# Fused chunked attention and gated MLP: other ranks in the second phase of an instruction planner

## The chip, the cores and the metric

The kernel runs on one core of a Trainium2 chip. A core has five engines with instruction queues of their own: PE (TensorE, matmuls into PSUM), DVE (VectorE), ACT (ScalarE), POOL (GpSimd) and SP (SyncE, which issues most of the DMAs here). They wait for each other by semaphores only, and each works through its own queue in order. The metric is the device time of one execution in microseconds (us), as the median over runs.

## The reference

For each of 4 batches and 8 heads (768 positions, head width 64), queries in chunks of 32 attend to 8 memory keys and to a window of 56 keys around the chunk. The result, as x of 768 x 512 per batch, goes through a gated MLP:

```
h = np.maximum(x @ w_in, 0.0)                      # 512 -> 1024
u, v = (h[..., :d_ff // 2], h[..., d_ff // 2:])
v_n = (v - mu) / np.sqrt(var + 1e-06)              # over the 512 features
v_s = np.einsum('ts,bsd->btd', w_spatial, v_n) + b_spatial[None, :, None]
out = (u * v_s) @ w_out                            # 512 -> 512
```

## The kernel before, in words

Every large product is made of three matmuls with operands that are split into a rounded high part and the low rest (high x high, low x high, high x low). ACT writes the high part (a CAST), DVE the low one (a subtraction of the high part from the operand).

**First phase.** Attention runs in 24 units of 128 queries, and among them the products with w_in (`f`). v_n and u go out to DRAM (`vn_far`, `u_far`).

**Second phase.** For each batch b, `spatial(b)` forms the 768 x 768 product with w_spatial and `ffn_o(b)` the product with w_out. Each is done on quarters of its operands by seven products instead of eight, p1 to p7 (the function `product`). A left operand is either a quarter itself (p1, p2, p4) or a sum of quarters (`sm`, function `total`, on DVE: s1 and s2 for p5 and p6, s3 for p7, s4 for p3). `left` then makes the operand `op` out of it: `high` on ACT, `low` on DVE. The steps of a spatial product run as p1, p2, p6, p5, p7, p4, p3, each of two parts of nine matmuls of 384 columns; those of ffn_o as p1, p6, p5, p7, p4, p3, p2, each of three parts of six matmuls of 256 columns. Between batches they alternate: after p1 (and p2) of spatial(b) comes ffn_o(b-1), then the rest of spatial(b).

The bank `y` gathers p1, p6, p7 and p4 one on the other: after each of them something has to read it before PE may add the next. In spatial these readers are: a bias add on DVE and a copy to `st` on ACT after p1, copies on ACT after p6 and p7, a multiplication into `ug` on DVE after p4. Results of p2, and of p5 with p3, lie in banks of the ring `f` (three of them), and DVE joins them to the copies in `st`. POOL adds a bias step to some of the `st` tiles and multiplies them into the gate tiles `ug` (the loaded u). The gated `ug` quarters are the operands of ffn_o.

**w_out.** It comes as float64, and `from_f64` turns it into float32 tiles `big` during the first phase. Then `right_hand` makes the seven right operands of ffn_o for each half c: two direct ones, and two sums on POOL per temporary tile `st` (eight 128 x 256 sums in all, L916); `split` writes a high part on ACT (L887) and a low part on DVE (L891) for each. `w_out_pair(c, rank, load_rank)` does this for one half.

**What sets the order.** No engine's order is written down. Each piece is given to `Plan.op` with an engine, an estimated duration, the keys it reads and writes, and a rank. `Plan.order` walks through estimated time: for each engine it takes, of the operations that are ready, the one that could start first, and among equal starts the one with the lowest rank. The result is one fixed list per engine. In the second phase ranks are `1e3 + seq[0]`, where `seq[0]` counts the steps given to the plan so far; PE's are `1e4 + seq[0]`. The two calls of `w_out_pair` stand right behind the first step of spatial(0).

Of the kernel before, what the change touches and what calls it, by code (L numbers as in the profile page):

```python
# [28 lines left out]
class Plan:  # L29
# [38 lines left out]
    def order(self):  # L68
        ops = self.ops
        users = [[] for _ in ops]  # L70
        left = [len(o[3]) + len(o[8]) for o in ops]
        for n, o in enumerate(ops):
            for d in (*o[3], *o[8]):
                users[d].append(n)
        end, ready = self.end, self.start = {}, {}
        free = {e: 0.0 for e in ENGINES}
        pipe, landed = self.landing, []
        lone = both = 0.0
        taken = {ring: [] for ring in self.rings}
        waiting = {e: [] for e in ENGINES}  # L80
        for n, o in enumerate(ops):
            if not left[n]:
                ready[n] = 0.0
                waiting[o[0]].append(n)
        out, spares = [], []
        while len(out) < len(ops):
            best = None
            for e, ns in waiting.items():
                pick = None
                for n in ns:  # L90
                    t = max(free[e], ready[n], free["POOL"] if ops[n][9] else 0.0, lone if e == "POOL" else 0.0)
                    if ops[n][5]:
                        t = max(t, self.held_by(landed, ops[n][5], 0))
                    for s in ops[n][7]:
                        have = taken[s[0]]
                        if s not in have and len(have) >= self.rings[s[0]]:
                            old = self.slots[have[-self.rings[s[0]]]]
                            t = max([t] + [end.get(m, 1e9) for m in old])
                    if t >= 1e9:
                        continue  # L100
                    late = max(t, free[e])
                    c = (late, ops[n][4], n)
                    if pick is None or c < pick:
                        pick = c
                if pick and (best is None or pick < best[0]):
                    best = (pick, e)
            (t, _, n), e = best
            if e == "PE" and self.idle and 9.0 < t < 36.0:
                spare = int((t - max(free[e], 9.0) - 0.7) / 0.225)
                if spare > 0:  # L110
                    spares.append((max(free[e], 9.0), -spare))
            _, us, _, _, _, mb, tail, held, _, alone, drag, shared = ops[n]
            beside, pace = {"DVE": (free["POOL"] if shared else 0.0, 1.75), "POOL": (both, 1.4)}.get(e, (0.0, 1.0))
            if beside > t:
                us += min((beside - t) * (1 - 1 / pace), us * (pace - 1))
            for s in held:
                if s not in taken[s[0]]:
                    taken[s[0]].append(s)
            waiting[e].remove(n)
            free[e] = t + us  # L120
            if alone:
                lone = t + us
            if shared:
                both = t + us
            if mb:
                pipe = max(pipe, t + us) + mb * drag / self.rate
                end[n] = pipe + self.landing
                landed.append((end[n], mb))
            else:
                end[n] = t + us + tail  # L130
            self.start[n] = t
            out.append((t, n))
            for m in users[n]:
                left[m] -= 1
                if not left[m]:
                    ready[m] = max([self.start[d] + ops[d][1] if ops[d][0] == ops[m][0] == "PE" else end[d] + self.lat for d in ops[m][3]]
                                   + [self.start[d] for d in ops[m][8]])
                    waiting[ops[m][0]].append(m)
        return [n for _, n in sorted(out + spares)]
# [19 lines left out]
def tile_chunked_attention_gmlp(  # L159
# [380 lines left out]
    seq = [0]  # L540
# [112 lines left out]
    def product(kind, b, steps, halves, chunks, width, parts, N, right, right_keys, sum_eng, done):  # L653

        tag = (kind, b)
        (a11, k11), (a12, k12), (a21, k21), (a22, k22) = halves
        W = chunks * width

        def total(name, in0, in1, o, keys, to=None):
            rank = 1e3 + seq[0]  # L660
            sm = ("sm", (*tag, to or name))

            def go():
                if to is None:
                    alloc("sm", sm[1], [P, W], F32)
                a = t_[sm].rearrange("p (s n) -> p s n", s=chunks)
                {"DVE": nc.vector, "POOL": nc.gpsimd}[sum_eng].tensor_tensor(a, in0(), in1(), op=o)  # L667
            op(sum_eng, dve(W) if sum_eng == "DVE" else pool_(W), go, r=keys, w=[sm], rank=rank,
               shared=sum_eng == "DVE")
            return (lambda: t_[sm].rearrange("p (s n) -> p s n", s=chunks)), [sm]  # L670

        def left(name, of, keys):
            rank = 1e3 + seq[0]
            ok = ("op", (*tag, name))

            def half(x):
                return t_[ok][:, x].rearrange("p (s n) -> p s n", s=chunks)

            def high():
                alloc("op", ok[1], [P, 2, W], F32R)  # L680
                nc.scalar.copy(half(0), of())  # L681

            def low():
                nc.vector.tensor_tensor(half(1), of(), half(0).bitcast(F32), op=ALU.subtract)  # L684
            op("ACT", act(W), high, r=keys, w=[(*ok, "h")], rank=rank)
            op("DVE", dve(W), low, r=[*keys, (*ok, "h")], w=[(*ok, "l")], rank=rank, shared=True)
            return half, [(*ok, "h"), (*ok, "l")]

        def blocks(name, a, bi, bank, first):
            half, keys = a  # L690
            for p in range(parts):
                n = (*tag, bank, p)
                ring = "y" if bank == "y" else "f"
                cols = slice(p * P, (p + 1) * P)

                def go(n=n, ring=ring, cols=cols):
                    o = alloc(ring, n, [P, N], F32, psum=True) if first else t_[ring, n]
                    m = 0
                    for s in range(chunks):
                        h, l_ = half(0)[:, s, cols], half(1)[:, s, cols]  # L700
                        rh, rl = right(bi, 0, s), right(bi, 1, s)
                        for x, y in ((h, rh), (l_, rh), (h, rl)):
                            m += 1
                            nc.tensor.matmul(o, x, y, start=first and m == 1, stop=m == 3 * chunks,  # L704
                                             skip_group_check=True)
                op("PE", 1e-3 * 3 * chunks * (0.4375 * N + 6.5), go, r=[*keys, *right_keys(bi)], w=[(ring, n)],
                   rank=1e4 + seq[0], tail=0.25)
                done(name, p, (ring, n))
            seq[0] += 1

        direct = {"p1": ("a11", a11, k11), "p2": ("a12", a12, k12), "p4": ("a22", a22, k22)}
        s1 = s2 = None
        for name in steps:
            if s1 is None and name not in direct:
                s1 = total("s1", a21, a22, ALU.add, [*k21, *k22])
                s2 = total("s2", s1[0], a11, ALU.subtract, [*s1[1], *k11])
            of = direct.get(name)
            if name == "p5":
                of = ("s1", *s1)
            elif name == "p6":  # L720
                of = ("s2", *s2)
            elif name == "p7":
                of = ("s3", *total("s3", a11, a21, ALU.subtract, [*k11, *k21]))
            elif name == "p3":
                of = ("s4", *total("s4", a12, s2[0], ALU.subtract, [*k12, *s2[1]], to="s2"))
            i, bank = {"p1": (0, "y"), "p2": (1, "x"), "p3": (2, "z"), "p4": (6, "y"), "p5": (3, "z"), "p6": (4, "y"),
                       "p7": (5, "y")}[name]
            blocks(name, left(*of), i, bank, name in ("p1", "p2", "p5"))
            yield
# [236 lines left out]
    for x in FIRST:  # L966
        if x[0] == "w":
            c = int(x[1])
# [31 lines left out]
    for b in range(B + 1):  # L1000
        if b < B:
            rank = 300.0 + 10 * b
# [6 lines left out]
                next(spatials[b])  # L1009
            if b == 0:  # L1010
                for c in range(2):
                    w_out_pair(c, 1e3 + seq[0], 180.0)
        if b:
            o = ffn_o(b - 1)
            if b == B - 1:
# [57 lines left out]
```

## Time and profile before

| | |
|---|---|
| median of 3 runs (range) | 378.03 us (375.24 to 379.47) |
| the profiled execution, its own time | 377.27 us |
| span of the profile in it | 375.5 us |
| PE busy in the span | 357.4 us, 95% |
| DVE, ACT, POOL busy | 290.7, 187.1, 157.0 us |

The profile shows one execution on the chip by the hardware profiler; its times count from the first instruction. Matmuls are pipelined and their ends are modelled, so the start of the next block tells better than the end of one when PE was through. "Granted clock" is the share of the full TensorE clock (2.4 GHz) that the matmuls got; the other level is 1.2 GHz. A number of DMAs, loads of weights into PE and semaphore work stand in queues of their own. A wait is put down to the release that came last.

### The profile page before, as it was taken

To read this page: it belongs to the slowest core of one execution; us is meant where nothing else is said; L and a number is where in the kernel's file an instruction comes from. 1 tells how busy PE (TensorE), PEld (TensorE's weight loads), DVE (VectorE), ACT (ScalarE), POOL (GpSimd) and SP (SyncE) were. 2 spreads that over 40 slices of the span, in tenths; PEclk is the share of its full clock that TensorE was granted. 3 is DMA by queue.
4 is the path that set the end of the run, shared out by engine and by line. 5 is a ranking of instruction groups with operands and counts; after the bars stand their busy time and mean duration, and the time that the engine had idled before them with its cause. 6 is when DMAs were issued, how large, how long until landed. Compare 5 with 4: busy or idle time off the path is not lost.

```text
span 375.5 us, 11922 instructions
## 1 busy us (share of the span) xinstructions
PE 357.4 (95%) x5026; PEld 330.2 (88%) x5026; DVE 290.7 (77%) x480; ACT 187.1 (50%) x334; POOL 157.0 (42%) x154
## 2 busy tenths in 40 slices
PE   2799999999999999999999997999999999999996
PEld 2787888988989889889798996999999999999995
DVE  3799977669577498574796789699969996898893
ACT  3568552555555446454473345336533742743271
POOL 6164643366286067620033486452256024207410
PEclk9999999999999999999999999899999999999999
DMA  8999987885796894977844444404720662140015
GB/s 203 259 237 251 226 248 246 257 250 161 216 261 200 237 265 140 244 191 223 264 138 147 176 160 178 161 1 150 265 93 1 185 236 86 65 147 1 0 44 168
DMA packets 47557, 65.52 MB, mean 174 GB/s; under 512 B 4496, under 2 KB 38928, under 8 KB 47504
## 3 DMA queue, kind: packets, MB, share of 16 engines
q1 hardware_dynamic: 46848, 64.44, 57.8%
q8 instruction: 39, 0.64, 0.7%
q10 hardware_dynamic: 656, 0.33, 0.3%
q14 instruction: 14, 0.11, 0.1%
HBM read 45.88 MB, written 18.87 MB: 172 GB/s over the span
## 4 chain that ended last, share of the span: by engine, by line
PE 79%; DVE 10%; DMA 6%; ACT 2%; SPq 1%; issue 1%; POOL 0%; DVEq 0%; ACTq 0%; POOLq 0%
PE y L704 21%; PE f L704 14%; PE f L554 11%; PE f L555 11%; PE f L556 10%; PE sx L412 8%; DMA big<-in_moe_w_in_dram 4%; PE xt L516 2%; PE pt L500 2%; DVE op L684 2%; DVE sm L667 2%; DMA vmain<-in_v_dram 2%; DVE wout L891 1%; SPq L281 1%; ACT op L681 1%
## 5 line engine op out<-in xcount | busy, mean ns | idle before, releaser
L704 PE MATMUL y<-wsp,op 128*128 128x384 f32 x288 | 53.9, 344 | 3.1 <-ACT op L681 2.1
L704 PEld LDWEIGHTS y<-wsp,op 128*128 128x128 f32 x288 | 51.4, 193 | 3.9 <-ACT op L681 2.4
L758 POOL TENSOR_TENSOR ug<-st,ug 128x384 f32<-128x384 f32 x24 | 34.5, 1452 | 34.8 <-DVE st L750 30.8
L554 PE MATMUL f<-x,win_h 128*128 128x384 f32 x128 | 45.8, 358 | 0.0
L556 PE MATMUL f<-x,win_h 128*128 128x384 f32 x128 | 43.2, 337 | 0.0
L555 PE MATMUL f<-x,win_l 128*128 128x384 f32 x128 | 43.1, 337 | 0.0
L554 PE MATMUL f<-win_h,x 128*128 128x512 f32 x96 | 41.0, 427 | 0.0
L704 PE MATMUL f<-wsp,op 128*128 128x384 f32 x216 | 39.4, 336 | 0.0
L555 PE MATMUL f<-win_h,x 128*128 128x512 f32 x96 | 38.0, 396 | 0.5 <-DVE x L525 0.3
L556 PE MATMUL f<-win_l,x 128*128 128x512 f32 x96 | 37.7, 393 | 0.0
L764 POOL TENSOR_TENSOR st<-st,bias 128x384 f32<-128x384 f32 x14 | 18.0, 1286 | 47.2 <-ACT st L744 33.5
L704 PEld LDWEIGHTS f<-wsp,op 128*128 128x128 f32 x216 | 37.6, 188 | 0.0
L684 DVE TENSOR_TENSOR op<-sm,op 128x768 fp32r<-128x768 f32 x32 | 34.0, 1066 | 3.8 <-ACT op L681 3.3
L704 PE MATMUL y<-wout,op 128*128 128x256 f32 x288 | 36.0, 281 | 0.4 <-DVE op L684 0.4
L452 DVE TENSOR_TENSOR xs<-sx,rec 128x512 f32<-128x512 f32 x24 | 16.5, 689 | 25.4 <-PE sx L412 25.2
L704 PEld LDWEIGHTS y<-wout,op 128*128 128x128 f32 x288 | 34.8, 188 | 1.0 <-DVE op L684 0.8
L590 POOL TENSOR_TENSOR rstd<-ve,mhalf 128x1 f32<-128x1 f32 x24 | 14.5, 604 | 49.4 <-DVE ve L586 47.5
L681 ACT CAST op<-sm 128x768 fp32r<-128x768 f32 x32 | 26.3, 837 | 16.5 <-DVE sm L667 16.1
L412 PEld LDWEIGHTS sx<-kmain,q 64*32 64x32 f32 x1536 | 17.2, 108 | 14.3 <-issue 11.7
L578 ACT ACTIVATE st<-f 128x512 f32<-128x512 f32 x24 | 14.3, 598 | 28.3 <-PE f L556 27.9
L412 PE MATMUL sx<-kmain,q 64*32 64x64 f32 x1536 | 21.1, 229 | 7.5 <-ACT kmain L397 7.5
L391 POOL COPY vmain<-memv 8x1024 f32<-8x1024 f32 x22 | 23.8, 1085 | 9.9 <-PE sx L412 7.7
(86 smaller groups left out, 777.5 us busy)
## 6 DMA issues: line engine op xcount, KB each, us to landing
vmain<-in_v_dram SPq DMA_DIRECT2D x48, 128.0 KB
u_far<-uo SPq DMA_DIRECT2D x32, 192.0 KB
vn_far<-st SPq DMA_DIRECT2D x24, 256.0 KB
vr<-vn_far SPq DMA_DIRECT2D x8, 768.0 KB
ug<-u_far SPq DMA_DIRECT2D x16, 384.0 KB
q<-in_q_dram SPq DMA_DIRECT2D x11, 512.0 KB
vmain<-in_v_dram SPq DMA_DIRECT2D x47, 96.0 KB
out_dram<-ot SPq DMA_DIRECT2D x33, 128.0 KB
```

The source lines that it names most:

```text
L391: ins = {"DVE": nc.vector, "POOL": nc.gpsimd}[eng].tensor_copy(to, of)
L412: ins = nc.tensor.matmul(o, w_, m, start=True, stop=True, skip_group_check=True)
L452: nc.vector.tensor_tensor(xs.rearrange("p t r d -> p r t d"), t_["sx", i][:, :, 1], rec.rearrange("p t r -> p r t").unsqueeze(3).broadcast ...
L554: nc.tensor.matmul(o, lh, rh, start=(j == 0), stop=False)
L555: nc.tensor.matmul(o, ll, rh, start=False, stop=False)
L556: nc.tensor.matmul(o, lh, rl, start=False, stop=(j == len(pairs) - 1))
L590: nc.gpsimd.tensor_tensor(a, t_["ve", i], mhalf, op=ALU.pow)
L681: nc.scalar.copy(half(0), of())
L684: nc.vector.tensor_tensor(half(1), of(), half(0).bitcast(F32), op=ALU.subtract)
L704: nc.tensor.matmul(o, x, y, start=first and m == 1, stop=m == 3 * chunks, skip_group_check=True)
L758: nc.gpsimd.tensor_tensor(g, t_[st(x)], g, op=ALU.mult)
L764: {"DVE": nc.vector, "POOL": nc.gpsimd}[eng].tensor_tensor(a, a, bias[:, 1], op=ALU.add)
```

## The change

Three edits.

```diff
@@ Plan.order: for each engine, the choice among ready operations
-                pick = None
+                pick, soon = None, []
...
                     late = max(t, free[e])
                     c = (late, ops[n][4], n)
+                    soon.append(c)
                     if pick is None or c < pick:
                         pick = c
+                if pick and e in ('ACT',) and pick[1] >= 1e3:
+                    pick = min((c for c in soon if c[0] <= pick[0] + 0.1), key=lambda c: (c[1], c[2]))
@@ product, total
-            rank = 1e3 + seq[0]
+            rank = 1e3 + seq[0] - 2
@@ main loop, b == 0
-                    w_out_pair(c, 1e3 + seq[0], 180.0)
+                    w_out_pair(c, 1e3 + seq[0] + (3, 5)[c], 180.0)
```

The sums of quarters (`total`) rank two steps earlier. The two halves of the w_out conversion rank three and five steps later. And where the plan would give ACT an operation of the second phase, it now takes the lowest rank among all that could start within 0.1 us of the first. No instruction is added, removed or resized. The instruction lists are the same up to the entry into the second phase (all attention, all products with w_in); from there on they differ in order. The lines of the changed file stand 3 higher.

**DVE, entry of the second phase.** Before, behind the bias add to the first part of p1 (y_3935). `sm_4083` is the sum s3, the operand of p7; L891 writes low parts of w_out, L750 joins p2 to its copy.

```order
L891 TENSOR_TENSOR wout_3958<-big_3358,wout_3958 128x256
L891 TENSOR_TENSOR wout_3958<-big_3373,wout_3958 128x2x256
L769 TENSOR_TENSOR y_3969<-y_3969,bias_100 128x384
L891 TENSOR_TENSOR wout_3958<-big_3459,wout_3958 128x256
L891 TENSOR_TENSOR wout_3958<-st_3961,wout_3958 128x2x256
L891 TENSOR_TENSOR wout_3958<-big_3495,wout_3958 128x2x256
L891 TENSOR_TENSOR wout_3958<-st_3979,wout_3958 128x2x256
L891 TENSOR_TENSOR wout_3958<-st_4001,wout_3958 128x2x256
L750 TENSOR_TENSOR st_3987<-f_3990,st_3987 128x384
L750 TENSOR_TENSOR st_4018<-f_4007,st_4018 128x384
L891 TENSOR_TENSOR wout_3958<-st_4038,wout_3958 128x2x256
L667 TENSOR_TENSOR sm_4083<-vr_3798 128x768
```

The same stretch in the change, from that bias add to the low part of p7's operand (`op_4002`):

```order
L772 TENSOR_TENSOR y_3935<-y_3935,bias_100 128x384
L670 TENSOR_TENSOR sm_3986<-vr_3798 128x768
L772 TENSOR_TENSOR y_3969<-y_3969,bias_100 128x384
L894 TENSOR_TENSOR wout_3958<-big_3358,wout_3958 128x256
L753 TENSOR_TENSOR st_3988<-f_3991,st_3988 128x384
L894 TENSOR_TENSOR wout_3958<-big_3373,wout_3958 128x2x256
L753 TENSOR_TENSOR st_4009<-f_4011,st_4009 128x384
L894 TENSOR_TENSOR wout_3958<-st_3961,wout_3958 128x2x256
L894 TENSOR_TENSOR wout_3958<-st_3979,wout_3958 128x2x256
L687 TENSOR_TENSOR op_4002<-sm_3986,op_4002 128x768
```

The sum s3 moved from behind eight low parts of w_out to the place right behind the first bias add; four of the eight now lie between it and p7's operand, and the other four come later.

**POOL and ACT, the same time.** On POOL all eight sums of w_out (L916) stood before the first gate; in the change (L919) five do, and three stand behind two gates and two bias steps:

```order
L919 TENSOR_TENSOR st_3979<-big_3373,st_3961 128x256
L761 TENSOR_TENSOR ug_3959<-st_3988,ug_3959 128x384
L761 TENSOR_TENSOR ug_3959<-st_4009,ug_3959 128x384
L767 TENSOR_TENSOR st_4054<-st_4054,bias_100 128x384
L767 TENSOR_TENSOR st_4071<-st_4071,bias_100 128x384
L919 TENSOR_TENSOR st_4004<-big_3495,st_4004 128x256
L919 TENSOR_TENSOR st_4101<-big_3495,big_3459 128x256
L919 TENSOR_TENSOR st_4101<-big_3495,st_4004 128x256
```

ACT in the change. `st_4114` and `st_4131` are the copies of the two parts of p7 that PE waits for before p4; `op_4117` is the operand of p1 of the next batch:

```order
L684 CAST op_4073<-sm_3908 128x768
L890 CAST wout_3958<-st_4004 128x2x256
L747 COPY st_4114<-y_3935 128x384
L684 CAST op_4117<-vr_4057 128x768
L747 COPY st_4131<-y_3969 128x384
L890 CAST wout_3958<-st_4101 128x2x256
```

A CAST of w_out, which reads the first of POOL's three late sums, now stands ahead of the copy that p4 waits for. Before, all of ACT's w_out work stood ahead of p7.

**DVE, ahead of ffn_o(0).** Before; `op_4173` is the operand of p1 of ffn_o(0), `sm_4162` and `sm_4202` its sums s1 and s2, and L769 the bias adds to p1 of spatial(1):

```order
L667 TENSOR_TENSOR sm_4162<-ug_3981,ug_3959 128x768
L750 TENSOR_TENSOR st_4051<-f_4055,st_4051 128x384
L684 TENSOR_TENSOR op_4159<-vr_4107,op_4159 128x768
L750 TENSOR_TENSOR st_4065<-f_4071,st_4065 128x384
L684 TENSOR_TENSOR op_4173<-ug_3963,op_4173 128x768
L769 TENSOR_TENSOR y_4177<-y_4177,bias_100 128x384
L667 TENSOR_TENSOR sm_4202<-sm_4162,ug_3963 128x768
```

In the change the same operand is `op_4172`:

```order
L670 TENSOR_TENSOR sm_4187<-ug_3981,ug_3959 128x768
L772 TENSOR_TENSOR y_4175<-y_4175,bias_100 128x384
L670 TENSOR_TENSOR sm_4201<-sm_4187,ug_3963 128x768
L772 TENSOR_TENSOR y_4189<-y_4189,bias_100 128x384
L687 TENSOR_TENSOR op_4172<-ug_3963,op_4172 128x768
```

The sum s2 and both bias adds now stand ahead of the operand that ffn_o(0) starts with. The same turn occurs in ffn_o(1): s2 ahead of p1's operand.

## Rows read from the trace of the kernel before

**Rows 1.** Timeline of PE: start, us, instructions; in brackets idle before and releaser.

```profile
221.75 3.28 PE L704 MATMUL f<-wsp,op 128*128 128x384 f32 x18
225.48 3.39 PE L704 MATMUL y<-wsp,op 128*128 128x384 f32 x18 [0.44 <-ACT st L744]
...
234.05 0.44 PE L704 MATMUL y<-wsp,op 128*128 128x384 f32 x1 [2.06 <-ACT op L681]
235.04 7.89 PE L704 MATMUL y<-wsp,op 128*128 128x384 f32 x35 [0.55 <-DVE op L684]
242.77 3.28 PE L704 MATMUL f<-wsp,op 128*128 128x384 f32 x18
...
252.13 4.37 PE L704 MATMUL y<-wout,op 128*128 128x256 f32 x36
...
258.44 4.36 PE L704 MATMUL y<-wout,op 128*128 128x256 f32 x36
...
273.07 6.40 PE L704 MATMUL y<-wsp,op 128*128 128x384 f32 x36
```

**Rows 2.** Windows, PE alone: length, busy (count), granted clock, DMA share, GB/s.

```profile
236.00:238.00 2.00, 2.00 (x9) 0.53 0.75 234
```

**Rows 3.** Chain that ended last: start, us, what.

```profile
231.46 1.69 DVE sm L667
233.17 0.84 ACT op L681
234.03 0.97 DVE op L684
```

**Rows 4.** Timeline of DVE and POOL around the first p6 operand.

```profile
220.11 1.23 DVE L684 TENSOR_TENSOR op<-sm,op 128x768 fp32r<-128x768 f32 x1 [0.90 <-ACT op L681]
...
222.04 1.47 POOL L916 TENSOR_TENSOR st<-big,st 128x256 f32<-128x256 f32 x1
...
222.82 1.50 DVE L684 TENSOR_TENSOR op<-sm,op 128x768 fp32r<-128x768 f32 x1
```

**Rows 5.** Timeline of DVE and POOL: pieces alone, and pieces that meet.

```profile
226.56 0.69 DVE L891 TENSOR_TENSOR wout<-st,wout 128x512 fp32r<-128x512 f32 x1
227.16 0.69 DVE L891 TENSOR_TENSOR wout<-big,wout 128x512 fp32r<-128x512 f32 x1
...
234.91 0.95 DVE L684 TENSOR_TENSOR op<-vr,op 128x768 fp32r<-128x768 f32 x1
...
241.06 1.02 POOL L764 TENSOR_TENSOR st<-st,bias 128x384 f32<-128x384 f32 x1 [0.70 <-DVE st L750]
241.16 1.74 DVE L684 TENSOR_TENSOR op<-vr,op 128x768 fp32r<-128x768 f32 x1 [0.18 <-ACT op L681]
242.16 1.62 POOL L758 TENSOR_TENSOR ug<-st,ug 128x384 f32<-128x384 f32 x1
...
246.16 0.56 DVE L750 TENSOR_TENSOR st<-f,st 128x384 f32<-128x384 f32 x1
```

**Rows 6.** Timeline of DVE: operands of p1 in ffn_o(0), of p7 in spatial(1).

```profile
246.64 1.26 DVE L684 TENSOR_TENSOR op<-ug,op 128x768 fp32r<-128x768 f32 x1
...
269.84 1.55 DVE L684 TENSOR_TENSOR op<-sm,op 128x768 fp32r<-128x768 f32 x1
```

**Rows 7.** Timeline of ACT: a copy and a cast of w_out.

```profile
228.91 0.48 ACT L744 COPY st<-y 128x384 f32<-128x384 f32 x1 [0.65 <-PE y L704]
229.28 0.62 ACT L887 CAST wout<-st 128x512 fp32r<-128x512 f32 x1
```

**Rows 8.** Timeline near the end: DVE and PE in ffn_o(3).

```profile
352.83 2.64 DVE L684 TENSOR_TENSOR op<-ug,op 128x768 fp32r<-128x768 f32 x2
...
358.77 1.57 PE L704 MATMUL y<-wout,op 128*128 128x256 f32 x11 [0.43 <-DVE op L684]
```

**Rows 9.** Timeline of the SP queue and of POOL: a paced load, the first gates.

```profile
224.14 0.32 SPq L281 DMA_DIRECT2D ug<-u_far  x1
...
229.89 2.42 POOL L758 TENSOR_TENSOR ug<-st,ug 128x384 f32<-128x384 f32 x2
```

## The prediction

> **What bounds the kernel now.** I read the page's busy shares first: PE is busy 95% of the span, so the end moves only by what PE waits for, or by the clock it is granted. The timeline of PE then shows where it is not at pace. Three blocks of 18 matmuls follow each other without a wait from 242.77 to 252.13 [rows 1]: 9.36 us for 54 matmuls, 0.173 us each, 3.12 us a block. In w_out blocks it is 6.31 us for 54 (252.13 to 258.44), 0.117 each, 2.1 a step. Against this pace the entry of the second phase loses three things. p2 starts at 221.75, so p6 could start at 224.87, and starts at 225.48. p5 should then end about 231.9, but p7 starts at 234.05 after 2.06 us of idle time, does one matmul, and waits 0.55 us more; its other 35 matmuls (with p4) start at 235.04 [rows 1]. These 35 take 7.73 us, until 242.77, and not 6.07, because the granted clock falls to 0.53 in 236 to 238, that is, to the lower level, behind the idle time [rows 2]: 1.66 us. The chain of waits says what p7 waited for: the sum s3 on DVE (231.46, 1.69 us), then its cast on ACT, then the low part on DVE [rows 3]. Ahead of that sum DVE had all its low parts of w_out to do.
>
> **What PE could gain.** The change puts s3 right behind the first bias add. If nothing else were late, PE would run p6, p5, p7, p4 from 224.87 on at pace, 12.48 us, and start p3 at 237.35 instead of 242.77. That is 5.4 us: 0.6 before p6, 3.2 for the two waits with their rounding, 1.66 for the clock. The Trainium skill gives the time from one matmul to the next as columns over 2.4 GHz plus 2.5 ns (TensorE: Matmul & The Clock Gate, "Wait — 56ns, not 53.3ns?"), so 162.5 ns for 384 columns. The rows have 173; by the page's figure the clock term would be 2.0 us and not 1.66, and I keep the rows.
>
> **What DVE and POOL can deliver.** All of this holds only if DVE's list keeps up, and the moved work stays in it. So I price the list. Alone, a 768-wide DVE instruction on SBUF tiles lets the next start after 0.88 us (234.03 to 234.91) [rows 3, 5]; a 512-wide low part of w_out after 0.60 (226.56 to 227.16), a 256-wide one I estimate from these at 0.33; a join out of PSUM takes 0.56 and I count 0.47 until the next. A POOL piece of 384 alone takes 1.02. When they meet, they wait in turn: POOL starts at 241.06 and ends at 242.08; the DVE piece that starts at 241.16 needs 1.74, ending at 242.90; the next POOL piece starts at 242.16 and needs 1.62, ending at 243.78 [rows 5]. Each time, the one in progress ends and the other then takes its usual time less some start (0.82 to 0.9). The join at 246.16 (0.56) does not take part, although POOL is busy with a gate. So SBUF pieces of the two engines count one after the other, with 0.92 for POOL's 384 and about 0.62 for its 256 (222.04 to 223.51, after waiting for about 0.8 of another) [rows 4].
> The Trainium skill speaks against this change in the same sense: the pair of SBUF ports that DVE and POOL share is an exclusive lock and no split of bandwidth (SBUF — State Buffer, "SBUF: two separate sides"). Taken as a split, the sum would be the first rival's.
>
> Walking the printed order with these prices:
> - **Start.** POOL's last three sums no longer run at 220 to 223.5, so the three DVE pieces from 220.11 (s4 between two low parts, 1.23 to 1.50 each [rows 4]) go at 0.88. The first bias add starts at 222.75 instead of 224.32. ACT's copy ends by 223.9, and p6 starts at 224.87, in time.
> - **p7.** s3 ends at 224.2, its cast at 225.0. Then DVE does a bias add, four low parts of w_out and two joins, and POOL's two gates and first bias step come between. The low part of p7's operand ends at 230.9, and PE wants it at 231.1. No wait, so no clock loss.
> - **p4.** ACT's cast of w_out stands ahead of p7's copy and needs POOL's first late sum, which comes behind two gates and two bias steps, each in turn with a DVE piece: 233.2. Cast (0.62) and copy (0.48) [rows 7] make it about 234.35, where PE is at 234.2: 0.15 us lost.
> - **p3.** Its second part needs a join that DVE does behind a low part of w_out and the operand of p1 of batch 1, with POOL's bias step between: 239.65, where PE is at 239.06. 0.65 lost.
> - **ffn_o(0), p1.** Its operand now stands behind s2 and both bias adds. From 222.75 until its end the two lists hold nine 768-wide DVE pieces (7.9), two and six of w_out (4.3), ten POOL pieces of 384 (9.2) and three sums (1.9), 23.3 us, and 2.9 us in which only PSUM pieces run: 248.95. Before, the operand was ready at 247.90 (246.64 with 1.26 [rows 6]), 4.2 us ahead of PE. Now PE is there at 247.5: 1.5 lost, start at 249.0.
> - **ffn_o(0), p7.** Behind that operand come three more operands, two sums, two joins and two gates: its low part ends at 255.66, PE is there at 255.3, 0.4 lost. Start at 255.7 against 258.44: **2.75 us ahead**.
> - **Later batches.** These lists have as many pieces as before. The next place where DVE was close is p7 of spatial(1): its operand ended at 271.39 (269.84 with 1.55 [rows 6]) for a start at 273.07 [rows 1], 1.7 us of room. DVE is ahead by 1.55 and PE by 2.75, so 0.5 of it is left, and I count nothing.
> - **Tail.** In ffn_o(3) the sum s2 now comes between the two low parts that took 2.64. The second one ends about 1 us after PE wants it, and the wait of 0.43 that stood one step later goes [rows 8]. I take 0.3 lost, between 0 and 1.
>
> DMA costs nothing here: the same loads are issued, vr's a few us earlier, when s3 has read its tile.
> Sum: 5.4 - 0.15 - 0.65 - 1.5 - 0.4 = 2.7, less 0.3 at the tail: about 2.4 us. Against the profiled execution's own 377.27 us this gives 374.8; against the median, which is 0.76 above it, 375.6. I forecast **375.2 us**. The bounds of the give-backs are 0 (gain 5.4, 371.9 to 372.6) and all of the gain (377.3 to 378).
>
> **Rivals.**
> - **Little is given back** (20%). DVE and POOL meet less than in a walk that lets them alternate strictly, for a piece that finds the other engine waiting for a semaphore costs it nothing. For it: before, only part of POOL's pieces were stretched. Then PE keeps 5.4 less 0.3 and some of the 0.15: **372.4 us**. Against it: DVE has no idle time left in my walk.
> - **All is given back** (13%). s2 ahead of p1's operand costs about 1 us in ffn_o(1) and ffn_o(2) too, where I found room of over 2 us in the first, and the room of 0.5 at p7 of spatial(1) is used up: **377.2 us**, no change.
> - **Slower** (10%). ACT's queue: the copies of p7 wait behind a cast of w_out that waits for POOL. It decides if POOL's first gate is late. Before, it began at 229.89; as late as that again, the late sum ends at 229.89 + 4 x (0.92 + 0.88) + 0.6 = 237.7, p7's copy at 238.8, and PE, wanting p4 at 234.2, waits 4.5 us. The clock would fall again (1.7), p3 would end at about 248 instead of 245.9, 2 us behind: **379.5 us**. The wait turns the gain into a loss at about 236 for the cast. Against it: the fourth load of a gate tile was let go at 224.14, by pacing on the first ones [rows 9], so the first tile is there, and the join it needs is at 225.4.
>
> The forecast itself has 57%, 373.6 to 377.
>
> **Numbers.** The runs shown lie between 375.24 and 379.47, so about 1%, 3.8 us, is what a measurement can tell from no change; faster by 1% means below 374.25. Of the forecast's case about a quarter lies there, of the first rival nearly all: 0.14 + 0.18, so 0.33 faster. Slower by 1% means above 381.8, which only the third rival reaches, with scatter: 0.05. Within 1%: 0.62. The range takes in the first rival and the second: 372.3 to 378.2.
>
> **What would show it.** Right: PE goes from p5 to p7 without idle time, the granted clock stays at its upper level from 225 to 250, and PE starts ffn_o(0) around 249 behind a wait for a low part on DVE, with DVE nearly without gaps from 222 to 256. The first rival: that block starts by 247.2, with no wait on DVE. The third: PE waits for ACT's copy before p4. Wrong altogether: a change ahead of 218 us, where the lists are the same, or an operand that waits for a `vr` load.

## The result, and the profile after

| | before | after |
|---|---|---|
| median of the runs, us | 378.41 (375.24 to 379.52) | **374.56** (373.39 to 381.60) |
| ratio after / before | | **0.9893**, 95% interval 0.9860 to 0.9926 |
| profiled execution, us (span) | 377.27 (375.5) | 373.39 (371.6) |
| start of phase two (p1 of spatial(0)), us | 218.63 | 218.20 |
| start of the last block, us | 367.41 | 363.52 |
| **phase two, from the one to the other, us** | **148.78** | **145.32** |

Two of the nine executions after (380.02 and 381.60 us) fell into a slower state of the chip; the ratios and the counts of executions below leave such ones out. The forecast was 375.2 us, with 372.3 to 378.2 as its range. The last line of the table is the measure used below. Phase one varies from one execution to the next: the change leaves its lists as they were, and two traces of the changed kernel start phase two at 218.20 and at 219.97. Phase two repeats: 145.32 and 145.26 in these two. So of the 3.89 us by which the last block came earlier in the first trace, 0.43 are phase one's scatter, and 3.46 us belong to the change. This is measured against an execution of before in which the granted clock fell; the section on the clock shows that it does not fall in each of them.

In the rows PE is TensorE, DVE is VectorE, ACT is ScalarE and POOL is GpSimd. The timeline of PE after the change (start, us, then in brackets the idle time before and what ended it; every line number behind the planner is 3 higher) answers to [rows 1]:

```profile
221.32 3.28 PE L707 MATMUL f<-wsp,op 128*128 128x384 f32 x18
224.44 3.28 PE L707 MATMUL y<-wsp,op 128*128 128x384 f32 x18
227.56 3.28 PE L707 MATMUL f<-wsp,op 128*128 128x384 f32 x18
230.68 6.72 PE L707 MATMUL y<-wsp,op 128*128 128x384 f32 x36
237.24 3.54 PE L707 MATMUL f<-wsp,op 128*128 128x384 f32 x18
240.62 3.28 PE L707 MATMUL y<-wsp,op 128*128 128x384 f32 x18
243.74 3.28 PE L707 MATMUL f<-wsp,op 128*128 128x384 f32 x18
246.85 0.28 PE L707 MATMUL y<-wout,op 128*128 128x256 f32 x1
247.97 4.36 PE L707 MATMUL y<-wout,op 128*128 128x256 f32 x35 [0.83 <-DVE op L687]
252.16 2.26 PE L707 MATMUL f<-wout,op 128*128 128x256 f32 x18
254.26 4.76 PE L707 MATMUL y<-wout,op 128*128 128x256 f32 x36
258.86 4.40 PE L707 MATMUL f<-wout,op 128*128 128x256 f32 x36
```

p2, p6, p5 and p7 follow each other every 3.12 us: the waits ahead of p6 and p7 are gone. Behind them the starts show what was given back. A pair of blocks of 36 should take 6.24 us and takes 6.56 (230.68 to 237.24); p3 takes 3.38 where 3.12 is the pace; p1 and p6 of ffn_o(0) with the wait take 5.31 (246.85 to 252.16) for 4.20; p7 and p4 there 4.60.

The granted clock of PE (length, busy and count, clock, share of DMA, GB/s), which was 0.53 in the first of these windows [rows 2]:

```profile
236.00:238.00 2.00, 2.00 (x14) 1.00 0.04 18
225.00:250.00 25.00, 24.17 (x142) 1.00 0.36 125
```

It stays at the upper level, 2.4 GHz, through the whole entry. VectorE's busy time in 28 us of the entry, before, after, and in an experiment below in which GpSimd does less (one row from each kernel):

```profile
222.00:250.00 28.00, 23.67 (x31) 0.94 0.42 148
```

```profile
222.00:250.00 28.00, 27.97 (x34) 1.00 0.43 147
```

```profile
222.00:250.00 28.00, 26.88 (x37) 1.00 0.45 155
```

After the change VectorE has 0.03 us of idle time left in 28. The long waits of PE are gone, and the engine that feeds it is now full; the runs below show that the 2.1 us given back come from there. The long pieces of VectorE and what GpSimd does at the time:

```profile
226.22 2.46 DVE L894 TENSOR_TENSOR wout<-st,wout 128x512 fp32r<-128x512 f32 x2
228.61 1.77 DVE L687 TENSOR_TENSOR op<-sm,op 128x768 fp32r<-128x768 f32 x1
230.30 1.77 DVE L687 TENSOR_TENSOR op<-vr,op 128x768 fp32r<-128x768 f32 x1
...
246.97 0.94 DVE L687 TENSOR_TENSOR op<-ug,op 128x768 fp32r<-128x768 f32 x1
...
253.59 0.96 DVE L687 TENSOR_TENSOR op<-sm,op 128x768 fp32r<-128x768 f32 x1
```

```profile
225.32 2.82 POOL L761 TENSOR_TENSOR ug<-st,ug 128x384 f32<-128x384 f32 x2 [5.91 <-DVE st L753]
228.10 3.16 POOL L767 TENSOR_TENSOR st<-st,bias 128x384 f32<-128x384 f32 x2
231.22 1.46 POOL L919 TENSOR_TENSOR st<-big,st 128x256 f32<-128x256 f32 x1
```

A piece that takes 0.95 us alone takes 1.77 beside one of GpSimd's, as in [rows 5]. GpSimd's gates begin at 225.32 and not at 229.89 [rows 9]. The rows of 246.97 and 253.59 are the low halves that p1 and p7 of ffn_o(0) wait for, and the chain of waits ends its part at the entry there (start, us, what):

```profile
253.59 0.97 DVE op L687
254.56 0.04 issue
254.60 4.41 PE y L707 x35
```

At the other end the wait of 0.43 us [rows 8] has moved one block ahead and is 0.65 us long:

```profile
351.97 0.28 PE L707 MATMUL f<-wout,op 128*128 128x256 f32 x1
352.90 2.25 PE L707 MATMUL f<-wout,op 128*128 128x256 f32 x17 [0.65 <-DVE op L687]
```

### The profile page after: what moved, and what is told of

Read it like the earlier page. It is cut to its first block, busy times and chain, and to the rows that moved or that the text cites. A ratio compares the mean times of both kernels' runs of the same rounds, so it can differ in the third digit from the quotient of the medians.

```text
span 371.6 us, 11928 instructions
## 1 busy us (share of the span) xinstructions
PE 356.2 (96%) x5026; PEld 328.6 (88%) x5026; DVE 294.7 (79%) x480; ACT 186.9 (50%) x334; POOL 157.1 (42%) x154
## 5 line engine op out<-in xcount | busy, mean ns | idle before, releaser
L707 PE MATMUL y<-wsp,op 128*128 128x384 f32 x288 | 52.4, 337 | 0.0
L707 PEld LDWEIGHTS y<-wsp,op 128*128 128x128 f32 x288 | 49.9, 188 | 0.4 <-ACT st L747 0.3
L687 DVE TENSOR_TENSOR op<-sm,op 128x768 fp32r<-128x768 f32 x32 | 36.6, 1144 | 2.0 <-ACT op L684 1.8
```

## The experiments

The theory: p7's wait and the clock behind it cost 5.4 us; putting s3 ahead of the low halves of w_out takes them away; what comes back is VectorE's full queue, stretched by GpSimd. The rivals: the three edits share the gain; the clock's term is not real; each wait behind the entry has a price of its own; VectorE is long by its own load.

All traces in one table. "Entry" runs from p1 of spatial(0) to the block of p3 and p2 of ffn_o(0); the 14 blocks in it take 38.58 us at pace (nine of 3.12 and five of 2.10).

| kernel | phase two starts | entry | phase two | timed ratio to before (95%) |
|---|---|---|---|---|
| before | 218.63 | 44.00 | 148.78 | |
| the change | 218.20 | 40.66 | 145.32 | 0.9893 (0.9860 to 0.9926) |
| the change, again | 219.97 | 40.62 | 145.26 | 0.9940 (0.9909 to 0.9971) |
| w_out's rank alone | 221.23 | 40.55 | 145.81 | 0.9922 (0.9887 to 0.9957) |
| the sums' rank alone | 219.44 | 44.26 | 148.97 | 1.0022 (0.9986 to 1.0059) |
| both ranks, no wait of ScalarE | 218.50 | 39.62 | **144.36** | **0.9864** (0.9817 to 0.9910) |
| before, PE kept busy | 218.41 | 42.47 | 147.25 | 0.9996 (0.9962 to 1.0030) |
| the same, again | 218.64 | 42.45 | 147.10 | 0.9981 (0.9950 to 1.0012) |
| small second bias | 219.73 | 38.58 | 143.20 | 0.9900 (0.9866 to 0.9934) |
| p1's operand first | 218.91 | 41.26 | 146.07 | 0.9964 (0.9934 to 0.9993) |
| bias on VectorE | 218.48 | 40.24 | 144.86 | 0.9928 (0.9897 to 0.9959) |
| sums of w_out on VectorE | 219.86 | 39.29 | 144.73 | 0.9880 (0.9841 to 0.9920) |
| both on VectorE | 221.31 | 40.79 | 145.43 | 0.9941 (0.9912 to 0.9969) |

The timed ratios carry phase one's scatter of up to 3 us (in the trace of w_out's rank alone, which starts phase two at 221.23, the granted clock averages 0.99 over the first 218 us and not 1.00); where they and the traces speak of differences below 1 us, only the traces tell them apart.

**Which edit does it.** w_out's rank alone (the other two undone):

```
-            rank = 1e3 + seq[0] - 2
+            rank = 1e3 + seq[0]
...
-                if pick and e in ('ACT',) and pick[1] >= 1e3:
-                    pick = min(...)
```

> Of the change's three edits only one is kept: the conversion of w_out takes ranks 3 and 5 higher. TensorE's order of work is then that of the kernel before, and on VectorE the sum s3, from which p7 of spatial(0) is made, stands ahead of all low halves of w_out that come from sums. Theory A (p7's wait was the whole matter, and this edit alone takes it away): 3.0 to 4.2 us faster than before, ratio 0.989 to 0.992; the 2.06 and 0.55 us waits ahead of p7 are gone, and the granted clock between 225 and 250 us is 1.00. The short wait ahead of p6 (0.44 us) may stay, since two low halves still stand ahead of p6's bias add. Rival B (the three edits share the gain, each giving about a third): 1.0 to 1.8 us faster, ratio 0.995 to 0.9975, a wait of 1 us or more left ahead of p7.

2.97 us of the 3.46, at a ratio of 0.9922: theory A, with its size just under the 3.0 expected. Its entry, 40.55 us, is as short as the change's 40.66. Of what is missing behind it, about 0.5 us are no wait: in this trace blocks that follow each other without one start 3.17 and 3.18 us apart (266.02, 269.19, 272.37) where 3.12 is the pace at a granted clock of 1.00. Why is open. Both waits ahead of p7 are gone, and the one of p6 too, although two low halves still stood ahead of its bias add in the plan.

The sums' rank alone (w_out's rank and ScalarE's wait undone):

> Only the lower rank of the sums of operand quarters is kept. At the entry of the second phase VectorE's order stays as it was before: s3 of spatial(0) stands behind the low halves of w_out, whose rank is lower still. Theory A: the waits ahead of p7 stay (2 us and 0.5 us, granted clock about half right behind them), and the time is that of before within 0.8 us, ratio 0.998 to 1.002; some tenths of a microsecond can come from the tail, where TensorE's blocks stand in another order. Rival B (the edits share the gain): 1.0 to 1.8 us faster, ratio 0.995 to 0.9975.

Phase two 0.19 us longer than before, ratio 1.0022. The waits stand where they stood:

```profile
234.85 0.44 PE L704 MATMUL y<-wsp,op 128*128 128x384 f32 x1 [2.04 <-ACT op L681]
235.84 7.89 PE L704 MATMUL y<-wsp,op 128*128 128x384 f32 x35 [0.55 <-DVE op L684]
```

So the edits do not share the gain in thirds. w_out's rank makes it, and the sums' rank alone is worth nothing; what it does on top of w_out's rank is the next run.

The change without ScalarE's wait (only that edit undone):

> The change without its third edit: ScalarE does not wait for a lower rank; sums lower and w_out higher as in the change. ScalarE then converts p3's operand and some others one or two places earlier or later than in the changed kernel. Theory A (the third edit moves only work that has slack): within 0.5 us of the changed kernel, ratio to before 0.988 to 0.991. Rival B (the third edit carries part of the gain by getting copies out of the banks that VectorE and GpSimd wait for): 1 us or more slower than the changed kernel, ratio to before 0.992 to 0.995.

Neither. It is *better* than the change: phase two 144.36 us, 0.96 less, the shortest of the kernels that compute all, and the lowest timed ratio, 0.9864 (its interval still overlaps the change's). PE starts ffn_o(0) without a wait:

```profile
247.26 4.37 PE L704 MATMUL y<-wout,op 128*128 128x256 f32 x36
251.46 2.26 PE L704 MATMUL f<-wout,op 128*128 128x256 f32 x18
```

```profile
245.88 1.30 DVE L684 TENSOR_TENSOR op<-ug,op 128x768 fp32r<-128x768 f32 x1
...
252.85 0.96 DVE L684 TENSOR_TENSOR op<-sm,op 128x768 fp32r<-128x768 f32 x1
```

Counted from the start of phase two, the low half for p7 of ffn_o(0) begins at 34.35 us here and at 35.39 with the change: 1.04 us earlier, and the entry is 1.04 us shorter. On top of w_out's rank alone, the sums' rank then gives 1.45 us (145.81 to 144.36), or about 1.0 without the slower repeat of products in that trace, and ScalarE's wait, which was not run without the other two edits, takes 0.96 away. From the first bias add to the start of that operand VectorE works through the same 35 pieces in both traces, in another order and with at most 0.13 us idle: 31.04 us with the change, 30.01 without ScalarE's wait. So the 1.04 us lie in the length of the pieces. That they are long where they meet GpSimd's rests on the runs below, which change GpSimd's part.

**The price of the clock.** The kernel before, with PE kept busy while it waits for p7's operand:

```
+            if (kind, b, name) == ("s", 0, "p7"):
+                def keep():
+                    o = alloc("y", "keep", [P, N], F32, psum=True)
+                    for _ in range(12):
+                        nc.tensor.matmul(o[:, 0:P], ident, ident, start=True, stop=True)
+                op("PE", 2.0, keep, r=[("f", ("s", 0, "z", 1))], w=[("y", "keep")], ...)
```

> The kernel before, with twelve products of the identity matrix with itself, 128 columns each, put into TensorE's stream between p5 and p7 of spatial(0); they are written to a bank of PSUM that nobody reads. All other engines keep their order, and p7 must wait for its operand as before. At 0.22 us each they fill 2.6 of the 3.05 us from the end of p5 to the second product of p7. Theory A (the low granted clock behind the wait costs time of its own, put at 1.66 us): the 35 products of p7 and p4 take 6.2 to 6.5 us in place of 7.89, the granted clock stays at 0.9 or above, and the kernel is 1.2 to 1.8 us faster than before, ratio 0.995 to 0.997. Rival B (whatever p7 and p4 lose is given back at the next wait, or the low clock is a matter of the profiled run alone): ratio 0.999 to 1.001.

> The kernel before with the twelve products of the identity ahead of p7 once more. In its trace phase two was 147.25 us in place of 148.78, as the clock's price of 1.5 us wants it, but the timed runs gave a ratio of 0.9996 with an interval down to 0.9962. Theory A (the low clock costs 1.5 us, the timed runs scatter by phase one): phase two 147.1 to 147.4 us again, ratio 0.994 to 0.998. Rival B (the trace of one execution was a lucky one): phase two 148 us or more, or a ratio above 0.999 with an interval that leaves out 0.996.

The traces agree with theory A twice: phase two 1.53 and 1.68 us shorter, with p7's operand no earlier. The rows of the second (each of the twelve products shows as two instructions):

```profile
231.84 2.84 PE L718 MATMUL y<-ident 128*128 128x128 f32 x24
234.44 0.42 PE L704 MATMUL y<-wsp,op 128*128 128x384 f32 x1
235.06 6.34 PE L704 MATMUL y<-wsp,op 128*128 128x384 f32 x35 [0.19 <-DVE op L684]
241.23 3.28 PE L704 MATMUL f<-wsp,op 128*128 128x384 f32 x18
```

```profile
236.00:238.00 2.00, 2.00 (x14) 1.00 0.71 240
```

The 35 products start at 235.06, where they started before (235.04 [rows 1]), and are done 1.56 us sooner, at a granted clock of 1.00 and not 0.53. The timed ratios, 0.9996 and 0.9981, lie nearer to no change, the first within rival B's numbers; the first interval leaves out the 0.9959 that 1.53 us would be, the second takes it in.

The mean granted clock, which is on record for every timed execution, says why. 1.66 us lost at half the clock lower the mean over 375.5 us by 0.0044, and the trace of before has 0.995. In the three sets of before's executions that were timed beside the experiments, 50 of 73 have 0.995 or less and the other 23 have 0.999 or more. Set by set, those at 0.994 or 0.995 took 1.2, 1.7 and 1.6 us longer on average than those at 0.999 or more. With the twelve products, 3 of 21 executions have 0.995 or less. So the fall of the clock costs about the same in timed executions, but it comes in two thirds of them at most. By these shares keeping the clock up is worth an estimated 0.8 us in the mean, a ratio of 0.998, which both intervals take in. At which place the clock fell is on record for the traces alone.

**What gives back.** The changed kernel with four of GpSimd's additions made small, all orders the same:

```
+                    w_ = slice(0, 8 if b == 0 else HT)
-                    ...tensor_tensor(a, a, bias[:, 1], op=ALU.add)
+                    ...tensor_tensor(a[:, w_], a[:, w_], bias[:, 1, w_], op=ALU.add)
```

> The changed kernel; in batch 0 GpSimd's four additions of the second bias work on 8 of the 384 columns (the other columns of those four tiles miss their bias: the part of the computation that is left out). Every engine keeps its order of work instruction by instruction. Phase two, from the first block of p1 of spatial(0) to the start of the last block, took 148.78 us in the trace of before, 145.32 in that of the change. Theory A (from 219.7 to 254.5 us VectorE's queue has no gap and is stretched by GpSimd: a piece of the one that works in SBUF alone stops one of the other): VectorE's four pieces beside those additions shrink by 0.9 us each, the operand of p1 of ffn_o(0) is there by 245 us in place of 247.9, the waits of TensorE at the entry (0.32, 0.26, 1.0 and 0.40 us against the pace) go nearly all, phase two takes 143.3 to 143.8 us, 1.5 to 2.0 us less than with the change. Rival B (VectorE's long pieces are slow by themselves or by the transfers of that time, GpSimd is not what stretches them): 145.0 to 145.6 us.

Theory A, and to the end: the entry takes 38.58 us, the pace of PE itself, with no wait left in it, and phase two 143.20 us. VectorE's rows, to be set against 228.61 and 230.30 of the change:

```profile
230.12 0.95 DVE L687 TENSOR_TENSOR op<-sm,op 128x768 fp32r<-128x768 f32 x1
231.00 0.95 DVE L687 TENSOR_TENSOR op<-vr,op 128x768 fp32r<-128x768 f32 x1
...
245.36 0.95 DVE L687 TENSOR_TENSOR op<-ug,op 128x768 fp32r<-128x768 f32 x1
```

```profile
229.62 1.52 POOL L768 TENSOR_TENSOR st<-st,bias 128x8 f32<-128x8 f32 x2
...
238.33 0.20 POOL L768 TENSOR_TENSOR st<-st,bias 128x8 f32<-128x8 f32 x1
```

The same two pieces, 0.95 us each and not 1.77; and two additions of 8 columns keep GpSimd for 1.52 us beside them, where another, which began while VectorE read PSUM, took 0.20. Each engine waits for the other's piece to end. The operand of p1 of ffn_o(0) was ready at 26.58 us into phase two (29.71 with the change). All of what the change gave back, 2.08 us of the entry, went with these four additions: it was GpSimd's share in VectorE's queue.

The changed kernel, with the sums of ffn_o(0) at their old rank, so that p1's operand there stands ahead of s2:

```
-            rank = 1e3 + seq[0] - 2
+            rank = 1e3 + seq[0] - (2 if tag != ("o", 0) else 0)
```

> The changed kernel, but the sums of operand quarters of ffn_o(0) alone keep their old rank. On VectorE the low half of p1's operand of ffn_o(0) then stands two sums and one bias addition further ahead; the total of work ahead of p7's operand of ffn_o(0) stays. Theory A (the terms of the entry are not a sum: VectorE's queue up to p7's operand of ffn_o(0) sets the time, and the 1.0 us wait at p1 is a part of the same debt, paid early): the wait at p1 of ffn_o(0) is gone or below 0.3 us, the block of p4 and p7 there loses 1.0 us or more in its place, phase two takes 145.1 to 145.6 us (145.32 with the change). Rival B (each wait has its own price, as the prediction added them up): 1.0 us less, 144.2 to 144.5 us.

Neither number. The wait at p1 went and came back at once, ahead of p6, whose operand is made from s2:

```profile
247.57 2.26 PE L707 MATMUL y<-wout,op 128*128 128x256 f32 x18
250.90 2.40 PE L707 MATMUL y<-wout,op 128*128 128x256 f32 x18 [1.07 <-ACT ot L812]
...
255.98 4.35 PE L707 MATMUL y<-wout,op 128*128 128x256 f32 x35 [0.47 <-DVE op L687]
```

p6 adds to the bank of p1, so ScalarE has to copy p1's result out first. That copy began at 250.48, behind the two casts of the operands made from s2 and s1, and these did not begin before 249.01, after s2, moved behind p1's operand, was done (248.62). Rival B, a price for each wait, falls: the one taken away gave nothing. But theory A, by which the total of the queue alone counts, is too simple as well: VectorE now waited 0.79 us for the first of those casts, and the entry ended 0.6 us later than with the change.

The second bias of batch 0 on VectorE (no wait of ScalarE):

```
-                eng = "DVE" if x in ("u3",) and b == B - 1 else "POOL"
+                eng = "DVE" if b == 0 or x in ("u3",) and b == B - 1 else "POOL"
```

> The change without its third edit, and in batch 0 the four additions of the second bias are done by VectorE, not GpSimd. Phase two took 144.36 us in the run without the third edit. Theory A (a GpSimd piece that works in SBUF alone costs VectorE about 0.9 us where they meet, VectorE needs 0.47 us for the same addition): VectorE's queue ends up to 1.7 us earlier at p7 of ffn_o(0), and the waits left at the entry (0.57 us at p4 of spatial(0), 0.35 us at p7 of ffn_o(0)) go: 143.4 to 143.9 us, 0.5 to 0.9 us less. Rival B (what stretches VectorE is its own load): four additions more make it 1.9 us later, 145 to 146.3 us, slower than without them by 0.7 us or more.

The sums of w_out on VectorE (no wait of ScalarE):

```
-        right_hand("wout", ..., rank, "POOL", "DVE")
+        right_hand("wout", ..., rank, "DVE", "DVE")
```

> The change without its third edit, and the eight sums of quarters of w_out are done by VectorE, not GpSimd. Theory A (as in the run with the bias on VectorE): a sum of 256 columns takes GpSimd 1.05 to 1.46 us and VectorE about 0.33 us, so VectorE gains on each that met it; the last halves of w_out no longer wait for GpSimd, and phase two takes 143.4 to 144.4 us (144.36 without this edit). Four sums now stand ahead of the operand of p7 of spatial(0); by my walk along the order it is there at 229.5 us, in time. Rival B (VectorE's own load is what counts): eight times 0.33 us later, a wait of up to 1 us ahead of p7 of spatial(0) again, 145.5 to 147 us.

Both:

> The change without its third edit, with both the second bias of batch 0 and the sums of w_out on VectorE; GpSimd has only the gates left at the entry. Theory A (GpSimd's pieces are what stretches VectorE's queue): 4 times 0.47 and 8 times 0.33 us of VectorE's own replace 12 pieces of GpSimd that cost it up to 0.9 us each; the operand of p7 of ffn_o(0) is there in time, phase two takes 143.3 to 144.2 us (144.36 without these two edits). Rival B (what counts is what stands in VectorE's queue ahead of each operand, whoever's work it was): waits of 0.3 to 0.8 us ahead of p7 and p3 of spatial(0), as with the bias alone on VectorE, 144.6 to 146 us.

144.86, 144.73 and 145.43 us against 144.36. Each of the first two misses both of its expectations. In the trace of the bias on VectorE the low half for p7 of ffn_o(0) begins at 33.65 us into phase two, 0.7 earlier than without the edit, so the queue as a whole did get shorter, as theory A says. Yet PE waits 0.29 and 0.82 us for the operands of p7 and p3 of spatial(0), for the planner had put the additions ahead of them, where the first two took 1.10 and 1.09 us beside GpSimd's sums and not the 0.47 counted; PE then reaches ffn_o(0) late by itself. The sums on VectorE shorten the entry by 0.33 us, and lose 0.7 us in later batches, whose order the planner also changed. Both together take rival B's time, but with a single wait of 1.65 us ahead of p3 and none ahead of p7:

```profile
242.02 3.27 PE L704 MATMUL f<-wsp,op 128*128 128x384 f32 x17 [1.65 <-DVE op L684]
```

So in these runs moving GpSimd's work to VectorE did not pay: what VectorE got stood ahead of the next operands, or the order changed later on. Lists in which neither happens were not tried.

The change once more, for the spread of the two phases:

> The changed kernel once more, beside the next run, to see how far the length of phase two (first block of p1 of spatial(0) to the start of the last block) repeats between executions while the length of phase one does not. If it is set by the order of the work: 145.2 to 145.5 us again (145.32 in the first trace), with the start of p1 anywhere from 218 to 221 us. If differences of a microsecond in phase two are chance: outside 144.8 to 145.8 us.

Phase two 145.26 us, phase one 1.8 us longer than in the first trace: the order sets the one, chance the other. The second set of runs had a median of 375.22 us.

## Why the prediction was right, step by step

| step | predicted, us | measured, us |
|---|---|---|
| gain by the start of p3 at pace | 5.4 | 5.42 |
| of it the granted clock | 1.66 | 1.53 and 1.68 in traces; in timed runs in two thirds of the executions at most |
| lost at p4 | 0.15 | 0.32 |
| lost at p3 | 0.65 | 0.26 |
| lost at p1 of ffn_o(0) | 1.5 | 1.11 |
| lost at p7 of ffn_o(0) | 0.4 | 0.40 |
| later batches and tail | 0.3 lost | 0.1 gained |
| net | 2.4 | 3.46 |

(Measured: 24.14 us before and 19.04 after, from p1 to p3, are 5.10, with the 0.32 of p4 5.42, which is before's time above the pace; the others from the starts shown, against 3.12 and 2.10 us a block. The last line of losses is the net less the rest.)

- **The mechanism** was right at p7 and behind it: PE ran from p5 into p7 without idle time, the clock stayed at its upper level, VectorE had next to no gap, and PE waited for a low half at the start of ffn_o(0). The gross 5.4 is read off before's trace, so it had to come out once the waits went; what was at stake is that they went.
- **The step at p4** had the wrong cause. The walk put its loss down to the cast of w_out that waits for GpSimd's late sum. In the trace that cast began at 232.71, and the copy behind it was done at 233.71, in time for PE at 233.80. PE waited for the second copy of p7, which stood behind a cast that waited for a load:

```profile
234.31 0.83 ACT L684 CAST op<-vr 128x768 fp32r<-128x768 f32 x1 [0.60 <-DMA vr<-vn_far]
235.05 0.47 ACT L747 COPY st<-y 128x384 f32<-128x384 f32 x1
```

  So "DMA costs nothing here" does not hold at p4, where the load cost about a quarter of a microsecond. An operand that waits for a `vr` load was named as a sign of being wrong altogether; here ScalarE waited for one, and PE for the copy behind it. In the second trace of the change that cast did not wait: p4 lost 0.07 us there and p3 0.51. The split is not fixed, but the sum is, 0.58 us in both: the second part of p3 waits for a join on VectorE and starts 20.75 us into phase two in both traces.
- **The size of the give-backs** was too large by 1.0 us in sum, most of it in three terms. The walk let the lists end at 248.95 for p1's operand; it was ready at 247.91, 248.34 on before's clock of phase one. Strict turns between VectorE and GpSimd overstate what they cost each other: GpSimd was idle for stretches of over a microsecond between its pieces, and some of its pieces met reads of PSUM. The tail was taken as 0.3 lost; the wait of 0.43 us there went, and that of 0.65 came in its place, while some 0.15 us were saved at ffn_o(2), where a block of 4.51 us before took 4.37, which the prediction did not see. The rival "little is given back" named the reason that made the net larger, but not the extent: 2.1 of 5.4 did come back.
- **The third edit** has no term of its own. The walk took the printed order as given, with all three edits in it, and so could not tell them apart. The cast ahead of p7's first copy stands there without this edit too; p4 then loses 0.68 us, so the edit helps at p4 and costs more later. In all it is worth 0.96 us, against the change.
- **The time.** 375.2 was forecast; the two sets of runs gave 374.56 and 375.22 us. The net of the trace would have put it 1 us lower; the scatter of phase one is as large as that error. That the forecast came within 0.7 us of both medians is in part luck.

## What to carry to other kernels

When a wait goes because one engine's list was put in another order, ask whether that engine has any gap left: if not, the rest of the gain is set by the sum of its list up to the last operand of the stretch, and moving one operand ahead only moves the wait. Price that list with the other engine's pieces in it, and take the edits apart before keeping all of them: here one edit made the gain and one took a part of it back. Where runs scatter by a first stage that the change does not touch, compare the length of the stage it does touch.

## What the runs showed of the hardware

- A VectorE and a GpSimd piece that both work on SBUF alone take turns whatever the size: two additions of only 8 columns held GpSimd for 1.52 us beside VectorE's low halves, and 0.20 us where one began beside a read of PSUM. The Trainium skill calls it an exclusive lock for the whole instruction (SBUF — State Buffer, "SBUF: two separate sides"), and these rows agree.
- Twelve idle products in a wait of 3 us kept the granted clock at 1.00 where it had been 0.53, and the next 35 products were done 1.56 us sooner. Without them the mean granted clock of before was 0.995 or less in 50 of 73 timed executions, with them in 3 of 21.
- The length of phase two repeated to 0.06 us in one kernel and 0.15 us in another, while the start of phase two lay anywhere from 218.20 to 221.31 us.
